# Two-step weight transfers, four token-halved projection units and a split step 1 in a one-core SSM + GeGLU kernel

## The chip, the cores and the metric

One core of a Trainium2 chip. The metric is the device time of one execution in microseconds (us), the median over several executions. Every execution also has a **span**: from the program's first instruction to its last, as the trace has it. Time less span is what lies outside.

Engines in profile lines: PE is TensorE, PEld its weight loads, DVE VectorE, ACT ScalarE, POOL GpSimd, SP SyncE, whose queue issues almost all transfers.

## The reference, cut to what matters

```python
x  = A_x                                   # (1, 2048, 512), bf16
xn = layernorm(x)                          # over the 512 columns
# A: a diagonal complex recurrence over the 2048 tokens
Bu = xn @ B_bar.T                          # the "B projection", 512 complex states
h_t = Lam_bar * h_{t-1} + Bu_t
y  = 2 * Re(h @ C.T) + xn * Dskip
# B: gated feed-forward, F = 1376
f  = (gelu(xn @ w_gate) * (xn @ w_up)) @ w_down
out = x + y + f
```

The kernel works on four blocks of 512 tokens, each of four 128-token tiles. A contraction over 512 columns takes four steps k = 0 to 3 of 128.

## The kernel before

A list of operations goes through a small scheduler in the program. It keeps the written order on TensorE and SyncE and sorts VectorE, ScalarE and GpSimd by its own model of time, so a change in one place can reorder those three.

The head: block 0 is computed from centred, not yet normed tiles, so that TensorE can start as soon as one tile and one weight step are there. SyncE sends tile x0, then single weight steps of 128 KB, with x2 and x3 between:

```python
def ld_wk(W, Wc, src, k):                                  # one step of one matrix
    f0, f1 = FC[0]                                         # columns 0 to 511
    return S.dma(lambda e: e.dma_start(W.ap[:, k, f0:f1], src[128*k:128*(k+1), f0:f1]),
                 256*(f1-f0), writes=[Wc[k]], tag="ld_w")
...
ld_x0(0)
GATE["par"] = S.order_behind(ld_x0(1, "scalar", [wrm]), GATE["table"])   # x1 on ScalarE's queue
for k in range(KD):
    if k in (1, 3):
        ld_x0((k + 3) // 2)
    ld_wk(WG, WGc, ins["B_w_gate"], k)
    ld_wk(WU, WUc, ins["B_w_up"], k)
ld_w(WG, WGc, ins["B_w_gate"], 1); ld_w(WU, WUc, ins["B_w_up"], 1)
... # then the last columns, the transpose of the parameters, the transposes of block 0
```

TensorE's order in the head; `ks(k, tile, which)` does step k of a tile for gate (0), up (1) or both, and `cent_T` transposes a centred tile:

```python
ks(0, 0, [0], True); ks(0, 0, [1])
cent_T(1, 1, 4, 7)
ks(0, 1, [0], True); ks(0, 1, [1])
ch(*stats(0, 2)); ch(sub(2))          # VectorE: statistics and centring of tile 2
ks(1, 0, [0, 1])                      # step 1 of tile 0
cent_T(2, 0, 1, 6); cent_T(2, 1, 4, 7)   # transposes of tile 2
ks(1, 1, [0, 1])
...
```

Later, the B projection of block 1 waits for the four transposes of that block's normed tiles. Its first units start on the first two tiles:

```python
def BU(b, halved=0):
    ...
    for unit_ in units[:halved]:
        mm(*unit_, 0, 2)                       # tokens 0 to 255
    for n, (c, s, bank) in enumerate(units):
        mm(c, s, bank, 2 if n < halved else 0, 4)   # the rest, or the whole unit
        ...                                    # eviction on ScalarE
...
BU(0); CHAIN(0, 2); H0_T()
BU(1, 2)
```

## Time and profile before

| | before |
|---|---|
| median of the first 3 runs | 177.25 us (176.85 to 177.71) |
| the execution whose trace the prediction read | 177.77 us, span 176.5 |
| TensorE busy | 97% |
| holes in TensorE's stream after 4.7 us, in that trace | 0.61 us and 0.72 us |

The profile lines, and how they are read, stand in the prediction.

### The profile page before, as it was taken

The page shows a single profiled execution, that of the slowest core. Times are in us where ns is not written, and L with a number is a line of the kernel's source. Part 1 is how long each engine was busy: PE and PEld are TensorE (multiplying, and loading weights), DVE is VectorE, ACT ScalarE, POOL GpSimd, SP SyncE. Part 2 cuts the span into 40 slices and gives each one's busy share as a digit, 9 for nine tenths or more (in the row PEclk, how much of TensorE's full clock was granted, in tenths as well). Part 3 has the DMA queues.
Part 4 walks back from the last instruction along what each step waited for, and adds up shares of the span by engine and source line. Part 5 has one row for each costly group of instructions (what it writes and reads, how often), then busy time and mean ns, then how long its engine had stood idle before and what let it go on. Part 6 is the DMA issues. An engine that isn't in the chain of part 4 may idle for free.

```text
span 176.5 us, 2485 instructions
## 1 busy us (share of the span) xinstructions
PE 172.0 (97%) x866; PEld 83.9 (48%) x881; DVE 159.8 (91%) x278; ACT 95.0 (54%) x187; POOL 9.8 (6%) x24
## 2 busy tenths in 40 slices
PE   8899999899999999999999999999999999999995
PEld 3545564544644444444644444444464444444454
DVE  6886999995999999879999999999999999999941
ACT  5464768799876899265676693000657970000000
POOL 3122040202000000000100000000000000000000
DMA  5899999895899000001134000002001000000312
GB/s 152 222 332 174 240 146 194 142 134 105 177 263 295 0 4 2 0 30 59 33 61 89 0 0 0 4 0 87 32 0 30 4 0 0 0 0 0 119 63 61
DMA packets 32420, 14.36 MB, mean 81 GB/s; under 512 B 23736, under 2 KB 32408, under 8 KB 32408
## 3 DMA queue, kind: packets, MB, share of 16 engines
q1 hardware_dynamic: 32240, 14.07, 36.7%
q8 instruction: 7, 0.11, 0.3%
q10 hardware_dynamic: 168, 0.13, 0.2%
q14 instruction: 5, 0.04, 0.1%
HBM read 6.46 MB, written 2.10 MB: 48 GB/s over the span
## 4 chain that ended last, share of the span: by engine, by line
PE 80%; DVE 6%; DMA 6%; SPq 4%; issue 2%; POOL 1%; DVEq 0%; POOLq 0%
PE PS L884 37%; PE PS L843 29%; PE PS L749 11%; DMA arena<-arena 6%; PE PS L817 2%; SPq L484 2%; DVE arena L599 1%; DVE arena L610 1%; SPq L489 1%; DVE arena L597 1%; DVE arena L629 1%; DVE arena L724 1%; SPq L493 1%; POOL arena L552 1%; DVE arena L864 0%
## 5 line engine op out<-in xcount | busy, mean ns | idle before, releaser
L884 PE MATMUL PS<-arena 128*128 128x512 bf16 (+3 forms) x317 | 65.9, 366 | 0.3
L843 PE MATMUL PS<-arena 128*128 128x512 bf16 x257 | 57.1, 379 | 0.4
L884 PEld LDWEIGHTS PS<-arena 128*128 128x128 bf16 (+1 forms) x323 | 30.8, 98 | 35.2
L843 PEld LDWEIGHTS PS<-arena 128*128 128x128 bf16 x264 | 25.8, 98 | 30.2
L787 DVE TENSOR_TENSOR_SCAN arena<-arena 128x512 bf16<-128x512 f32 x32 | 38.8, 1254 | 0.0
L858 ACT ACTIVATE arena<-PS 128x512 bf16<-128x512 f32 x33 | 19.8, 599 | 24.8 <-DVE arena L902 16.7
L749 PE MATMUL PS<-arena 128*128 128x512 bf16 (+1 forms) x134 | 28.2, 366 | 0.7 <-DMA arena<-arena 0.6
L862 ACT ACTIVATE arena<-PS 128x512 bf16<-128x512 f32 x33 | 19.8, 601 | 4.7 <-PE PS L843 4.7
L749 PEld LDWEIGHTS PS<-arena 128*128 128x128 bf16 x136 | 13.2, 98 | 14.9 <-DMA arena<-arena 0.8
L876 ACT ACTIVATE PS<-arena 128x512 f32<-128x512 bf16 (+2 forms) x17 | 9.6, 581 | 19.7 <-DVE arena L902 19.0
L758 ACT ACTIVATE arena<-PS 128x512 bf16<-128x512 f32 x32 | 17.6, 594 | 2.5 <-PE PS L749 2.5
L902 DVE TENSOR_TENSOR arena<-PS,arena 128x512 bf16<-128x512 f32 (+2 forms) x17 | 10.8, 652 | 6.3 <-PE PS L884 6.3
L864 DVE TENSOR_TENSOR arena<-arena 128x512 bf16<-128x512 bf16 x33 | 13.2, 417 | 2.2 <-ACT arena L862 2.0
L776 DVE TENSOR_TENSOR arena<-arena 128x4096 bf16<-128x4096 bf16 (+1 forms) x5 | 9.2, 1859 | 0.8 <-ACT arena L606 0.8
L774 DVE TENSOR_TENSOR arena<-arena 128x4096 bf16<-128x4096 bf16 (+1 forms) x5 | 9.2, 1859 | 0.3 <-ACT arena L605 0.3
L799 DVE TENSOR_TENSOR arena<-arena 128x4096 bf16<-128x4096 bf16 x4 | 9.1, 2287 | 0.1
L800 DVE TENSOR_TENSOR arena<-arena 128x4096 bf16<-128x4096 bf16 x4 | 9.1, 2283 | 0.0
L610 DVE BATCH_NORM_STATS2 arena<-arena 128x6 f32<-128x512 bf16 x12 | 7.7, 678 | 0.5 <-DMA arena<-in_A_x_dram 0.5
L721 ACT ACTIVATE arena<-PS,arena 128x256 bf16<-128x256 f32 (+1 forms) x16 | 6.1, 446 | 2.5 <-DVE arena L556 1.6
L712 PE MATMUL PS<-arena 128*128 128x512 bf16 (+1 forms) x40 | 7.1, 336 | 0.0
L724 DVE SCALAR_TENSOR_TENSOR arena<-PS,arena 128x256 bf16<-128x256 f32 (+1 forms) x16 | 6.3, 444 | 0.6 <-PE PS L701 0.6
L701 PE MATMUL PS<-arena 128*128 128x512 bf16 (+1 forms) x28 | 6.0, 348 | 0.4 <-issue 0.4
(95 smaller groups left out, 123.6 us busy)
## 6 DMA issues: line engine op xcount, KB each, us to landing
out_dram<-arena SPq DMA_DIRECT2D x15, 128.0 KB, 1.7
arena<-in_A_x_dram SPq DMA_DIRECT2D x3, 512.0 KB, 5.9
arena<-in_B_w_down_dram SPq DMA_DIRECT2D x1, 1280.0 KB, 7.0
arena<-in_B_w_gate_dram SPq DMA_DIRECT2D x4, 128.0 KB, 3.1
arena<-in_B_w_up_dram SPq DMA_DIRECT2D x4, 128.0 KB, 3.4
arena<-in_B_w_gate_dram SPq DMA_DIRECT2D x1, 480.0 KB, 6.9
arena<-in_B_w_up_dram SPq DMA_DIRECT2D x1, 480.0 KB, 7.8
arena<-arena SPq DMA_TRANSPOSE x25, 3.1
```

Of the source, the lines that this page charges most:

```text
L610: return (V(lambda e: e.bn_stats(ST[tt].ap, X[tt].ap), d_dve_1x(512), [X[tt]], [ST[tt]], "bnst"), V(lambda e: e.bn_aggr(MVt[b][j].ap, ST[t ...
L749: ins_ = e.matmul(PS[bank][:, 128 * j0:128 * j1], BBT[c][dk].ap[:, 128 * s:128 * (s + 1)], XNT[b].ap[:, dk, 128 * j0:128 * j1], start=(dk ...
L758: GATE["evBu"] = ACT(lambda e, bank=bank, k3=k3, s=s, c=c: e.activation(SSc[k3][s][c].ap, PS[bank][:, :], ACTF.Copy), d_act(512), [BANK[ba ...
L774: V(lambda e, s0=s0, s1=s1: e.tensor_tensor(TA.ap[:, s0:s1], ssb.ap[:, s0:s1], cos4[:, s0:s1], ALU.mult), d_dve_tt2x(1024 * step), [ss, CO ...
L787: V(lambda e, g=g, rb=rb, init=init: e.tensor_tensor_scan(g.ap, rb, g.ap, init, ALU.mult, ALU.add), d_dve_scan(512), [g, PA[RRr]] + ([CARc ...
L843: ins_ = e.matmul(PS[bank][0:m, c0:c1], W.ap[:, dk, 128 * ft:128 * ft + m], XNT[b].ap[:, dk, c0:c1], start=(dk == 0), stop=(dk == KD - 1))
L858: GATE["last_gelu"] = ACT(lambda e, bg=bg, kk=kk, m=m: e.activation(GG[kk].ap[0:m, :], PS[bg][0:m, :], ACTF.Gelu_apprx_tanh), d_act(512), ...
L862: ACT(lambda e, bu=bu, kk=kk, m=m: e.activation(UPB[kk].ap[0:m, :], PS[bu][0:m, :], ACTF.Copy), d_act(512), [BANK[bu]], [UPB[kk]], "evU")
L864: V(lambda e, kk=kk, m=m, ft=ft, k2=k2: e.tensor_tensor(HTt[k2][ft].ap[0:m, :], GG[kk].ap[0:m, :], UPB[kk].ap[0:m, :], ALU.mult), d_dve_tt ...
L876: ACT(lambda e: e.activation(PS[bank][:, c0:c1], X[tt].ap[:, c0:c1], ACTF.Copy), d_act(c1 - c0), [X[tt]], [BANK[bank]], "seed")
L884: ins_ = e.matmul(PS[bank][:, c0:c1], l_[:, 128 * j:128 * (j + 1)], r_[:, c0:c1], start=False, stop=last and n == len(ops) - 1, skip_group ...
L902: V(lambda e: e.tensor_tensor(OUTB[ko].ap[:, c0:c1], PS[bank][:, c0:c1], XD[tt].ap[:, c0:c1], ALU.add), d_dve_1x(c1 - c0), [BANK[bank], XD ...
```

## The change

Its intent: fewer issues on SyncE's queue, so that what comes behind the weights (parameters, transposes of blocks 0 and 1) starts earlier; more work for TensorE while the transposes of block 1 are on their way; and a start on step 1 with its gate half.

```diff
-def ld_wk(W, Wc, src, k):
+def ld_wk(W, Wc, src, k0, k1):            # steps k0 to k1-1 in one transfer, rearranged "(k p) f -> p k f"
...
-for k in range(KD):
-    if k in (1, 3):
-        ld_x0((k + 3) // 2)
-    ld_wk(WG, WGc, ins["B_w_gate"], k)
-    ld_wk(WU, WUc, ins["B_w_up"], k)
+ld_wk(WG, WGc, ins["B_w_gate"], 0, 2)
+ld_wk(WU, WUc, ins["B_w_up"], 0, 2)
+ld_x0(2)
+ld_wk(WG, WGc, ins["B_w_gate"], 2, 4)
+ld_wk(WU, WUc, ins["B_w_up"], 2, 4)
+ld_x0(3)
...
-ks(1, 0, [0, 1])
+ks(1, 0, [0])
+ks(1, 0, [1])
...
-BU(1, 2)
+BU(1, 4)
```

(The body of `ld_wk` is cut to a comment; the rest is whole.)

More of the change, by code (lines that the diff above doesn't have):

```diff
@@ L480, in ld_x @@
                 512 * 1024, writes=X[4 * b:4 * b + 4], tag="ld_x%d" % b)
-        def ld_wk(W, Wc, src, k):
+        def ld_wk(W, Wc, src, k0, k1):
             f0, f1 = FC[0]
-            return S.dma(lambda e: e.dma_start(W.ap[:, k, f0:f1], src[128 * k:128 * (k + 1), f0:f1]),
-                         256 * (f1 - f0), writes=[Wc[k]], tag="ld_w")
+            return S.dma(lambda e: e.dma_start(W.ap[:, k0:k1, f0:f1], src[128 * k0:128 * k1, f0:f1].rearrange("(k p) f -> p k f", p=128)),
+                         256 * (k1 - k0) * (f1 - f0), writes=Wc[k0:k1], tag="ld_w")
         def ld_w(W, Wc, src, n):
```

## The prediction

> **What bounds the kernel now.** I read the page's busy table and the chain that ended last, then TensorE's order of time, then the wait of each gap in it, then the DMA queue's order of time.
>
> Busy table and chain, of the page (share of the span 176.5 us):
>
> ```profile
> PE 172.0 (97%) x866; PEld 83.9 (48%) x881; DVE 159.8 (91%) x278; ACT 95.0 (54%) x187; POOL 9.8 (6%) x24
> ...
> PE 80%; DVE 6%; DMA 6%; SPq 4%; issue 2%; POOL 1%; DVEq 0%; POOLq 0%
> ```
>
> TensorE is busy 97% and carries 80% of the chain. A busy row says little about pipelined matmuls, so I went through TensorE's starts one by one. Next to one another, matmuls of 512 columns start 216 ns apart and those of 256 columns 109 ns. Against that spacing there are only two holes between 4.7 us and the end, apart from five gaps of exactly one matmul (0.216 us), which I take for missing records. They stand in the order of time (start, length, last column: idle before and what ended it):
>
> ```profile
> 5.33 0.60 PE L701 MATMUL PS<-arena 128*128 128x256 bf16 x4
> 6.38 0.59 PE L701 MATMUL PS<-arena 128*128 128x512 bf16 x2 [0.45 <-issue]
> ...
> 24.56 7.94 PE L749 MATMUL PS<-arena 128*128 128x512 bf16 x39
> 33.06 6.21 PE L749 MATMUL PS<-arena 128*128 128x256 bf16 x31 [0.56 <-DMA arena<-arena]
> ```
>
> The rows show modelled ends that include the drain. Start to start, hole 1 is 6.376 - 5.655 - 0.109 = 0.61 us, hole 2 is 33.061 - 32.233 - 0.109 = 0.72 us. After 33.06 us TensorE's stream is dense for 141.5 us, to 174.6. So whatever reaches 33 us earlier or later moves the end by the same amount, and a change that adds no work can win at most 0.61 + 0.72 = 1.33 us, or 0.75%. That already settles most of the question at a 2% mark.
>
> Who ends the holes? Hole 1 is the wait for the up half of weight step 1. The DMA view of the window 3.0 to 3.2 us has it (size, us from issue to landing); issued at 3.08, it landed at 6.28, and the matmul starts at 6.38:
>
> ```profile
> arena<-in_B_w_up_dram SPq DMA_DIRECT2D x1, 128.0 KB, 3.2
> ```
>
> Hole 2 is the wait for the transposes of block 1: issued at 24.89, 26.13, 27.46 and 29.17, they landed at 30.86, 31.36, 32.35 and 32.92.
>
> The queue's order of time, head and what follows, shows the cost of issuing:
>
> ```profile
> 5.45 0.44 SPq L484 DMA_DIRECT2D arena<-in_B_w_up_dram  x1
> ...
> 8.20 2.81 SPq L510 DMA_TRANSPOSE arena<-arena  x1
> 11.06 5.18 SPq L736 DMA_TRANSPOSE arena<-arena  x4
> 16.28 0.58 SPq L478 DMA_DIRECT2D arena<-in_A_x_dram  x1
> 16.91 3.09 SPq L521 DMA_TRANSPOSE arena<-in_A_B_re_dram  x1
> ```
>
> One load occupies the queue for 0.47 us, whether 128 or 384 KB. And VectorE, which the block-1 transposes depend on, has one hole there:
>
> ```profile
> 16.92 0.16 DVE L553 TENSOR_TENSOR arena<-arena 128x4 f32<-128x4 bf16 x1 [1.46 <-POOL arena L552]
> ```
>
> POOL's instruction waited for the parameter transpose, issued at 8.20 and landed at 15.66 behind the weights.
>
> **What the Trainium skill says.** "DMA: Bandwidth & Descriptors", Rules for kernel authors, advises coalescing small transfers, and its Anatomy section puts a fixed cost of about 2 us on a DMA, most of it the write receipt. The trace agrees on the size: the first 128 KB load took 2.2 us to land, the first weight load 2.4. The same page, Queues, rings and completion order, says descriptors on each DMA engine are consumed in ring order. So a tile issued behind larger weights starts after their bytes; landings in the head do follow issue order in this trace. "TensorE: Matmul & The Clock Gate", Back-to-back issue gap, gives N / 2.4 + 2.5 ns for warm matmuls: 216 and 109 ns, exactly what the trace has.
>
> **The change part by part.**
>
> (a) Four halved units instead of two. Before, eight 256-column matmuls on tokens 0 to 255 ran from 31.47 to 32.34, and then TensorE waited for transposes 3 and 4. With four units there are sixteen, 16 x 0.109 = 1.74 us, to 33.21 if the start is the same. The last transpose landed at 32.92, plus the 0.14 us seen from landing to matmul, so at 33.06: hole 2 closes whole. Cost: eight 512-column matmuls become sixteen of 256, 8 x (2 x 109 - 216) = 16 ns. The PSUM banks are free: the evictions of units 0 to 3 of block 0 ended by 28.81. Sum: -0.70 us.
>
> (b) Loads. Before, the queue sends x0, WG0, WU0, x2, WG1, WU1, WG2, WU2, x3, WG3, WU3; now x0, WG01, WU01, x2, WG23, WU23, x3. Four issues go, 4 x 0.474 = 1.9 us of queue time. Hole 1 must vanish as such: step 1 arrives with step 0. But x2 now lies behind 256 KB more. TensorE's next work after step 1 of tile 0 is the transpose of tile 2, and it needs x2, its statistics and its centring. In the trace x2 landed at 5.11 and the centred tile was done at 6.43, so 1.32 us later. With 0.04 to start, the tile-2 transposes can't start before X + 1.36, X being the new landing of x2. They started at 6.81. The head therefore gains 5.45 - X, capped at the 0.61 of hole 1 (with x2 unmoved it would be 0.34), and loses if X is later than 5.45.
>
> What is X? Bytes ahead of and with x2 (the second tile, from the other queue, included) grow from 640 to 896 KB. Packets in the trace reach 640 KB at 4.4 us and 896 KB at 5.3, and landing follows 0.7 us or more behind. The stretches of one microsecond (last columns: DMA share, GB/s) show how full the engines were:
>
> ```profile
> 2.00:3.00 1.00, 1.00 (x4) 0.43 (x3) 0.39 (x2) 0.21 (x2) 0.36 (x2) 1.00 1.00 342
> 3.00:4.00 1.00, 1.00 (x6) 0.33 (x5) 0.96 (x3) 0.72 (x2) 0.00 (x0) 1.00 0.67 167
> 4.00:5.00 1.00, 1.00 (x11) 0.73 (x10) 0.59 (x3) 0.46 (x3) 0.00 (x0) 1.00 0.90 308
> 5.00:6.00 1.00, 0.93 (x10) 0.60 (x8) 0.83 (x2) 0.95 (x3) 0.00 (x0) 1.00 0.88 190
> ```
>
> Only the stretch from 3 to 4 us has room, a third of it: at 342 GB/s, 0.33 x 342 = about 113 KB. If the larger transfers fill it, 896 KB are moved when 783 were, at about 4.85, and X is about 5.6 (4.85 + 0.75). If they fill nothing, X is about 6.1; if the engines kept 342 from 2 us on, it is 4.7 + 0.7 = 5.4. My middle is 5.6: the head loses 0.15 us.
>
> (c) The gate half of step 1 alone. Two 512-column matmuls become four of 256: 4 ns. Both halves of step 1 lie in transfers that the step 0 matmuls have already waited for, so I expect no gain from it.
>
> (d) The queue is freed 1.9 us earlier, but the parameter transpose that follows held it 2.81 us with the weights still draining, so I count 0.5 to 1 us for what comes behind it. VectorE's 1.46 us hole shrinks, so block 1 is normed and transposed earlier too. That only matters for hole 2, closed by (a) anyway. It counts nothing more.
>
> Sum: -0.70 + 0.15 = -0.55 us. Before, the median was 177.25, so **176.7 us**.
>
> **Rivals.** First: x2 lands much later (6.1 to 6.3). For it speak latencies growing from 2.2 to 3.7 us over the head, a sign of a backlog that larger transfers do not cure. Against it, the 0.67 share. Head loss 0.65 to 0.85, total about 177.25 to 177.4: no change. Second: the loads run at full rate and the head gains up to 0.3; then the halves would also come earlier, and TensorE would need transposes 1 and 2 of block 1 before 31.36. If they move with the queue, the total is about 176.2; if not, that gain turns into a wait ahead of the halves, and it is 176.55. Third: a new order on VectorE and ScalarE, since the program's own list scheduler sorts them again, opens a stall. Against it: block 0's states, ready at 69.8, are first needed near 74.1 (64.6 plus 44 matmuls of 216 ns), 4 us of slack; the first reused bank of block 1's projections is free at 44.1 and needed at 45.8. A microsecond of disorder is absorbed; 177.5 at worst.
>
> **Range and chances.** The mechanisms span 176.2 to 177.5, and three runs before spread over 0.9 us. 8 in 10: **176.0 to 177.5**. Faster by over 2% needs 3.5 us, and the holes hold 1.33: 0.01. Slower by over 2% needs a stall that nothing here shows: 0.015. Within 2%: 0.975.
>
> **What would show it.** Right: no TensorE idle before the second token halves of block 1, and thirty-two 256-column matmuls there; four weight loads of 256 KB with x2 landing near 5.6; idle ahead of the tile-2 transposes instead of ahead of step 1; parameter transpose landed before 15.66. Wrong: a new wait of over 0.5 us after 33 us, x2 after 6.3, block 1's transposes landing after 33.1, or a different dense length after the projections.

## The result, and the profile after

| | before | changed |
|---|---|---|
| median of 6 runs | 177.26 us (176.85 to 177.71) | 178.03 us (177.67 to 178.37) |
| span of the traced execution | 176.5 | 176.4 |
| time less span | 1.26 to 1.37 over 33 runs in later sessions | 1.67 to 1.78 over 6 runs |

The ratio is 1.0041, with a 95% interval of 1.0020 to 1.0063. A ratio is the mean time of one kernel's fast runs over that of the other's of the same rounds, so it is not quite the ratio of the medians. The changed kernel is **0.4% slower**, inside 2%, but outside the predicted range of 176.0 to 177.5, and with the other sign.

The odd thing first: the two traced spans are equal, yet the times of these two executions differ by 0.4 us (177.77 and 178.18). So part of the loss is not in the span at all.

The page of the changed kernel, busy row and chain:

```profile
PE 172.1 (98%) x876; PEld 85.0 (48%) x891; DVE 160.1 (91%) x278; ACT 95.3 (54%) x187; POOL 11.9 (7%) x24
...
PE 94%; DMA 2%; DVE 1%; SPq 1%; issue 1%
```

TensorE now carries 94% of the chain: the wait for transposes in the middle is gone from it. In TensorE's order of time (start, length, form, count, then idle before and its cause):

```profile
4.75 0.39 PE L702 MATMUL PS<-arena 128*128 128x256 bf16 x2
5.72 0.39 PE L702 MATMUL PS<-arena 128*128 128x256 bf16 x2 [0.58 <-DMA arena<-in_B_w_up_dram]
5.95 0.33 PE L680 MATMUL PS<-arena 128*128 128x128 bf16 x3
6.12 1.04 PE L702 MATMUL PS<-arena 128*128 128x256 bf16 x8
7.38 0.40 PE L680 MATMUL PS<-arena 128*128 128x128 bf16 x4 [0.23 <-DVE arena L951]
7.62 2.97 PE L702 MATMUL PS<-arena 128*128 128x512 bf16 x13
...
25.15 11.21 PE L750 MATMUL PS<-arena 128*128 128x512 bf16 x65
```

The wait ahead of step 1 is gone. In its place stand two others: 0.74 us start to start ahead of the up half of step 0, and 0.39 us ahead of the tile-2 transposes (the brackets show less, since modelled ends include the drain). In the kernel before, the same rows were:

```profile
6.81 0.38 PE L679 MATMUL PS<-arena 128*128 128x128 bf16 x4
7.03 2.97 PE L701 MATMUL PS<-arena 128*128 128x512 bf16 x13
```

The block of 13 large matmuls begins at 7.62 instead of 7.03 us: the head loses **0.59 us**. Against that, the projections run from 25.15 through with no hole. The last matmul starts at 174.26 instead of 174.36, a net gain of 0.10 us on this pair of traces.

VectorE shows who held the tile-2 transposes, and the DMA view of the window 2.1 to 2.2 us when its input came (size, us from issue to landing; issued at 2.17, so landed at 6.00):

```profile
6.03 0.69 DVE L611 BATCH_NORM_STATS2 arena<-arena 128x6 f32<-128x512 bf16 x1 [1.33 <-DMA arena<-in_A_x_dram]
```

```profile
arena<-in_A_x_dram SPq DMA_DIRECT2D x1, 128.0 KB, 3.8
```

In the kernel before, x2 was issued at 2.12 and landed at 5.11 (window 2.1 to 2.3 us):

```profile
arena<-in_A_x_dram SPq DMA_DIRECT2D x1, 128.0 KB, 3.0
```

The stretches of one microsecond (last two columns: DMA share, GB/s) show that the larger transfers did fill the gap from 3 to 4 us, 286 GB/s where the kernel before had 167; from 2 to 3 us they moved less, 284 for 342:

```profile
2.00:3.00 1.00, 1.00 (x4) 0.43 (x3) 0.52 (x2) 0.22 (x2) 0.36 (x2) 1.00 0.94 284
3.00:4.00 1.00, 1.00 (x6) 0.44 (x5) 0.96 (x3) 0.62 (x2) 0.00 (x0) 1.00 1.03 286
4.00:5.00 1.00, 1.00 (x10) 0.60 (x7) 0.51 (x3) 0.59 (x5) 0.00 (x0) 1.00 0.97 296
5.00:6.00 1.00, 0.42 (x5) 0.26 (x4) 0.00 (x0) 0.45 (x2) 0.00 (x0) 1.00 1.01 326
```

More bytes moved by 6 us, and still a later start: bandwidth was not what the head wanted.

SyncE's queue shows the issues saved, and what became of them:

```profile
5.88 0.86 SPq L489 DMA_DIRECT2D arena<-in_B_w_up_dram  x1
6.87 2.24 SPq L511 DMA_TRANSPOSE arena<-arena  x1
10.97 5.15 SPq L737 DMA_TRANSPOSE arena<-arena  x4
```

The parameter transpose is issued 1.3 us earlier (6.87 for 8.20) and lands at 13.36 instead of 15.66, but block 0's transposes start at 10.97 instead of 11.06. They wait for tile 0 to be normed, and VectorE, held up by x2, is 0.9 us later there. The first of them lands 2.2 us earlier (13.71 for 15.88), the last only 0.1 (17.36 for 17.47), and what the queue issues next starts 0.1 us earlier (16.17 for 16.28).

### The profile page after: what moved, and what is told of

It reads as the page before. It is cut to its first block, busy times and chain, and to the rows that moved or that the text cites. A ratio compares the mean times of both kernels' runs of the same rounds, so it can differ in the third digit from the quotient of the medians.

```text
span 176.4 us, 2498 instructions
## 1 busy us (share of the span) xinstructions
PE 172.1 (98%) x876; PEld 85.0 (48%) x891; DVE 160.1 (91%) x278; ACT 95.3 (54%) x187; POOL 11.9 (7%) x24
## 4 chain that ended last, share of the span: by engine, by line
PE 94%; DMA 2%; DVE 1%; SPq 1%; issue 1%
PE PS L885 37%; PE PS L844 32%; PE PS L750 16%; PE PS L713 4%; PE PS L818 3%; PE PS L702 2%; DMA arena<-in_A_x_dram 2%; SPq L484 0%; DVE arena L611 0%; PE PS L680 0%; SPq L493 0%; DVE arena L951 0%; DVE arena L903 0%; DVE arena L612 0%
## 5 line engine op out<-in xcount | busy, mean ns | idle before, releaser
L844 PEld LDWEIGHTS PS<-arena 128*128 128x128 bf16 x264 | 25.7, 98 | 30.3
L750 PEld LDWEIGHTS PS<-arena 128*128 128x128 bf16 x144 | 14.1, 98 | 13.3
```

Of the source, the lines that this page charges most:

```text
L750: ins_ = e.matmul(PS[bank][:, 128 * j0:128 * j1], BBT[c][dk].ap[:, 128 * s:128 * (s + 1)], XNT[b].ap[:, dk, 128 * j0:128 * j1], start=(dk ...
L844: ins_ = e.matmul(PS[bank][0:m, c0:c1], W.ap[:, dk, 128 * ft:128 * ft + m], XNT[b].ap[:, dk, c0:c1], start=(dk == 0), stop=(dk == KD - 1))
```

## The experiments

Three questions: where the 0.4 us outside the span come from, what the head loses and why, and what the four halves are worth.

**1. The loads without the four halves.**

```diff
 # the changed kernel
-BU(1, 4)
+BU(1, 2)
```

> The changed kernel with two halved B-projection units instead of four; VectorE's and ScalarE's order is then that of the kernel before. Theory (the head's bytes): x2 lands near 6.0 us and the 13 large matmuls after the tile-2 transposes start near 7.62 instead of 7.03, a loss of 0.59 us; the block-1 transposes land near 32.3 to 32.9, and TensorE, later by 0.59, ends its eight half matmuls at 32.93, so the wait ahead of the second halves shrinks from 0.72 to under 0.2. Span 176.4 to 176.6, so the four halves add little to these loads. Rival (the halves alone hid the wait): the wait stays at 0.7 and the span is near 177.1. Time outside the span: if the 0.5 us that the changed kernel has there come with its loads, they are here; if with the number of TensorE instructions, they are not.

Measured: median 177.84, ratio 1.0031 (1.0012 to 1.0049). In its trace, which is of the longest of the six runs, x2 landed at 6.41 and the up half of step 0 at 6.07, later than expected; the 13 large matmuls started at 8.02. The wait ahead of the second token halves is 0.20 us, where the rival had 0.7. Mean span of six runs 176.28, as in the changed kernel (176.32). So **with these loads the two more halves add next to nothing**. Time less span is 1.68 to 1.78: it comes with the loads, not with the number of TensorE's instructions or the orders on VectorE and ScalarE, which are here those of the kernel before (the traces have the same sequences).

**2. The four halves alone.**

```diff
 # the kernel before
-BU(1, 2)
+BU(1, 4)
```

> The kernel before with four halved B-projection units and nothing else. Theory: hole 1 (0.61 us ahead of step 1) stays, hole 2 (0.72 us ahead of the second token halves) closes, span 175.75 to 175.85, 0.70 us below the kernel before. Rival: the new order of VectorE and ScalarE, which the four halves bring with them, moves the wait elsewhere, and the span is above 176.2. Time less span: 1.3 us as before if the loads made the difference, 1.7 if the instruction counts did.

Measured: median 177.38 beside 177.37 of the kernel before; ratio 0.9994 (0.9973 to 1.0015). The trace has no hole left at all, hole 1 included, and a span of 175.6; but the six spans run from 175.5 to 176.9 with a median of 176.05, and those of the kernel before in the same session have a median of 176.0. Both theories miss: the hole was closed, and nothing was won. A gain of 0.70 us would be a ratio of 0.9961, below the interval. VectorE and ScalarE run in the order of the changed kernel here, so that order costs nothing that can be seen either. That made me doubt the hole. Time less span is 1.28 to 1.33.

**3. x2 on the other queue.**

```diff
 # the changed kernel
 GATE["par"] = S.order_behind(ld_x0(1, "scalar", [wrm]), GATE["table"])
+GATE["par"] = S.order_behind(ld_x0(2, "scalar", [wrm]), GATE["par"])
...
-ld_x0(2)
```

> The changed kernel with tile x2 sent from ScalarE's queue behind x1, ahead of the large weight transfers. Theory (bytes bound, not the queue's order alone): x2 lands before 4.8 us and no longer gates, but the up half of steps 0 and 1 then has 896 KB ahead of and with it and lands near 5.7 to 6.1, so TensorE waits 0.8 to 1.1 us there and the tile-2 transposes start near 7.1 to 7.4; the head still loses 0.3 to 0.6 us against the kernel before; span 176.0 to 176.4. Rival (x2's place in the queue is the whole cause): the head gains 0.3 to 0.6 us against the kernel before and the span is 175.1 to 175.5.

Measured: median 177.87, ratio 1.0043 (1.0011 to 1.0075). The up half of step 0 landed at 5.92, TensorE waited 1.03 us for it, the tile-2 transposes started at 7.23; the median span is 176.3 (five runs 176.1 to 176.7, one 178.3). As the theory has it: with 896 KB to move ahead of the last one needed, taking x2 forward only moves the wait to the weights. One number missed: x2 itself, issued at 1.43, landed at 5.37 and not before 4.8.

**4. Single first steps, x2 on the other queue.**

```diff
 # experiment 3
-ld_wk(WG, WGc, ins["B_w_gate"], 0, 2)
-ld_wk(WU, WUc, ins["B_w_up"], 0, 2)
+for k in range(2):
+    ld_wk(WG, WGc, ins["B_w_gate"], k, k + 1)
+    ld_wk(WU, WUc, ins["B_w_up"], k, k + 1)
```

> As e3, but steps 0 and 1 of both weights in transfers of one step (128 KB) and steps 2 and 3 in one of two, four halved units, gate half of step 1 alone. Theory: the first up half lands near 4.9 to 5.1, step 1's gate half near 5.4 and up half near 5.8; TensorE's waits before the tile-2 transposes add to under 0.3 us, those start near 6.3 against 6.81; no wait before the second token halves; span 175.1 to 175.4 (both holes of 1.33 us gone). Rival: the transposes 1 and 2 of block 1 become the gate and give 0.3 to 0.5 us back, span 175.5 to 175.8.

Measured: median 177.95, ratio 1.0026 (1.0010 to 1.0042). A miss: x2 landed at 5.42 and pushed the first up half, single again, to 5.64; TensorE waited 0.70 us there. Mean span 176.10, no better than before. Time less span 1.78 to 1.87, another value again.

**5. The changed kernel with a longer SyncE program.** Time less span had been 1.31 in kernels with 82 SyncE instructions in the trace, 1.71 with 78, 1.55 with 77 (experiment 3) and 1.83 with 79 (experiment 4). So I lengthened the program where SyncE idles:

```diff
 # the changed kernel, where the program emits its waits
+if op is self.out_ops[4]:                 # ahead of the fifth store
+    for _ in range(4):
+        h.wait_ge(*waits[-1])             # a wait that is already fulfilled
```

> The changed kernel with four more waits, already fulfilled, on SyncE ahead of its fifth store, where it idles: its count of instructions in the trace goes from 78 back to 82, that of the kernel before. Theory (the 0.4 us outside the span hang on the length of SyncE's program, not on the loads): time less span falls from 1.67 to 1.78 to about 1.33, the span stays at 176.0 to 176.6, and the median time is near 177.6. Rival (the loads themselves leave something open at the end): time less span stays at 1.7, median 178.0.

Measured: time less span **1.35 to 1.41**, from 1.67 to 1.78, with nothing else altered. Only two of the four waits appear in the trace: 80 instructions, not 82. The median is 177.8, ratio 1.0032, since the mean span of these six is 176.47. The loads leave little or nothing open at the end: 0.33 of the 0.40 us go when SyncE's program has two more instructions in the trace.

**6. Halves and gate half on the loads of before.**

```diff
 # the kernel before
-ks(1, 0, [0, 1])
+ks(1, 0, [0])
+ks(1, 0, [1])
...
-BU(1, 2)
+BU(1, 4)
```

> The kernel before with its loads of single steps, with four halved units and with the gate half of step 1 of tile 0 alone. Theory: with single transfers the gate half lands 0.3 to 0.85 us ahead of the up half, so it can run first and hole 1 shrinks by up to 0.22 us; the second hole is closed; span 175.4 to 175.9, time less span 1.33, median 177.0. Rival (the head's landing times vary from run to run by as much): no difference from e2, median 177.3.

Measured: median 177.17 beside 177.29; ratio 0.9996 (0.9982 to 1.0009). The rival: no difference that can be told from the scatter. In its trace TensorE ran at half speed until 6.5 us (see experiment 11), so there was no wait ahead of step 1 for the split to shorten.

**7. The kernel before with four more waits.** The edit of experiment 5 on the kernel before.

> The kernel before with four more fulfilled waits on SyncE (82 to 86 instructions). Theory (length of SyncE's program): time less span moves away from 1.33 by 0.1 us or more, in a direction I can't tell, with the span unchanged at 175.9 to 176.5. Rival: 1.33 stays. The run also gives a second trace of the head of the kernel before: I expect the two holes to be there in other sizes, 0.3 to 0.7 each, as spans of its runs lie between 175.9 and 176.5.

Measured: median 177.15, ratio 0.9993 (0.9981 to 1.0005); time less span 1.25 to 1.33, not moved. That part of the theory fell: a longer program does not always shift it. Together the counts give 77: 1.55, 78: 1.71 to 1.73 (three kernels), 79: 1.83, 80: 1.38 and 1.39 (two kernels with different loads), 82: 1.30 to 1.32, 84: 1.29 and 1.31. It rises by 0.1 to 0.2 per instruction up to 79 and then drops; the kernels of this row differ in other ways too, and only experiments 5 and 7 change the count alone.

The second half of the expectation was worth more. TensorE in this trace of what is, in the head and the middle, the kernel before:

```profile
4.75 1.01 PE L704 MATMUL PS<-arena 128*128 128x256 bf16 x4
5.55 0.52 PE L682 MATMUL PS<-arena 128*128 128x128 bf16 x3
5.88 1.39 PE L704 MATMUL PS<-arena 128*128 128x256 bf16 x6
7.10 0.39 PE L682 MATMUL PS<-arena 128*128 128x128 bf16 x4
7.32 2.97 PE L704 MATMUL PS<-arena 128*128 128x512 bf16 x13
...
24.86 11.41 PE L752 MATMUL PS<-arena 128*128 128x512 bf16 x59
```

The last row has the projections of blocks 0 and 1 in one piece: **there is no second hole**, with two halved units only. The transposes of block 1 landed at 29.25 to 31.88 instead of 30.86 to 32.92.

**8. The same bytes ahead of x2, in single transfers.**

```diff
 # the changed kernel
-ld_wk(WG, WGc, ins["B_w_gate"], 0, 2)
-ld_wk(WU, WUc, ins["B_w_up"], 0, 2)
+for W, Wc, nm in ((WG, WGc, "B_w_gate"), (WU, WUc, "B_w_up")):
+    for k in range(2):
+        ld_wk(W, Wc, ins[nm], k, k + 1)
```

> The changed kernel with the first two transfers of two steps split into four of one step in the same order of bytes (gate 0, gate 1, up 0, up 1, then x2). Theory (bytes ahead): x2 still lands at 5.9 to 6.4 us, the tile-2 transposes start at 7.3 to 7.7 as in the changed kernel; the up half of step 0 lands at 5.0 to 5.5, so the wait for it shrinks to under 0.5 us but the one for x2 grows. Span 176.2 to 176.7. Rival (the size of a transfer is what costs): x2 lands before 5.5 and the span falls to 175.9 or less.

Measured: median 178.22, ratio 1.0055 (1.0042 to 1.0068), mean span 176.86. TensorE's order of time:

```profile
4.74 0.40 PE L703 MATMUL PS<-arena 128*128 128x256 bf16 x2
5.38 0.39 PE L703 MATMUL PS<-arena 128*128 128x256 bf16 x2 [0.24 <-DMA arena<-in_B_w_up_dram]
5.61 0.33 PE L681 MATMUL PS<-arena 128*128 128x128 bf16 x3
5.78 1.04 PE L703 MATMUL PS<-arena 128*128 128x256 bf16 x8
7.39 0.40 PE L681 MATMUL PS<-arena 128*128 128x128 bf16 x4 [0.57 <-DVE arena L952]
```

x2 landed at 6.01 us, to a hundredth where the two-step transfers put it (6.00), and the tile-2 transposes start at 7.39 for 7.38. The view of the window 3.05 to 3.1 us has the tile, issued at 3.10:

```profile
arena<-in_A_x_dram SPq DMA_DIRECT2D x1, 128.0 KB, 2.9
```

The size of the transfers is not what delays the tile. **It is the 896 KB ahead of and with it** instead of 640. One thing missed: the mean span is 0.54 us longer than that of the changed kernel, above the expected 176.2 to 176.7. In the trace 0.29 us of it are two more gaps, after 8.7 and 10.4 us; the up half of steps 2 and 3 landed at 8.97 instead of 7.40. So nothing here speaks against two-step transfers as such.

**9. A version made from what was learned.** Single steps 0 and 1 with x2 in its old place, two-step transfers for 2 and 3 only, four halves, gate halves of two tiles first, and eight more waits on SyncE.

```diff
 # the changed kernel, and the waits of experiment 5, eight of them
-ld_wk(WG, WGc, ins["B_w_gate"], 0, 2)
-ld_wk(WU, WUc, ins["B_w_up"], 0, 2)
-ld_x0(2)
+for k in range(2):
+    ld_wk(WG, WGc, ins["B_w_gate"], k, k + 1)
+    ld_wk(WU, WUc, ins["B_w_up"], k, k + 1)
+    if k == 0:
+        ld_x0(2)
...
 ks(1, 0, [0])
+ks(1, 1, [0])
 ks(1, 0, [1])
 cent_T(2, 0, 1, 6); cent_T(2, 1, 4, 7)
-ks(1, 1, [0, 1])
+ks(1, 1, [1])
```

> Single transfers for steps 0 and 1 with x2 where the kernel before has it, transfers of two steps for 2 and 3 only, x3 after them, four halved units, the gate halves of step 1 of tiles 0 and 1 ahead of their up halves, and eight fulfilled waits on SyncE to keep its program at 80 or more. Theory: x2 lands near 5.1 with 640 KB ahead of and with it; the wait for step 1's up half falls under 0.3 us; two issues fewer bring the block-1 transposes forward; no second hole; span 175.5 to 175.8, time less span 1.3 to 1.4, median 176.9, faster than the kernel before by 0.1 to 0.3%. Rival: the new orders on VectorE and ScalarE, or steps 2 and 3 landing after 8.4 us, give it back; span 176.0 and over, no gain.

Measured: median 177.76, ratio 1.0034 (1.0012 to 1.0055), mean span 176.53, time less span 1.26 to 1.36. The rival: x2 landed at 5.54 instead of 5.1; the wait for step 1 is gone, but the up half of steps 2 and 3 landed at 8.42 and the stream has small gaps of 0.15 and 0.16 us around there. The orders on VectorE and ScalarE also changed, and the trace does not say which of the two costs most. It beats neither the kernel before nor experiment 6.

**10. The kernel before, once more.** Unchanged, one look. A single run has no state; its clock was 1.0.

> The kernel before, unchanged, for a second trace. Theory (the trace that the prediction read was of an off-median execution, its second hole larger than is usual): the transposes of block 1 land at 30 to 32.3 us instead of 32.92 and the wait ahead of the second token halves is under 0.4 us; span 175.7 to 176.2. Rival: the hole is again 0.6 to 0.8 us.

Measured: 177.10, span 175.8. The transposes landed at 29.52 to 31.65, and again there is no second hole:

```profile
6.05 0.59 PE L701 MATMUL PS<-arena 128*128 128x512 bf16 x2 [0.15 <-issue]
6.67 0.40 PE L679 MATMUL PS<-arena 128*128 128x128 bf16 x4
6.91 3.03 PE L701 MATMUL PS<-arena 128*128 128x512 bf16 x13
...
24.51 11.84 PE L749 MATMUL PS<-arena 128*128 128x512 bf16 x62
```

Hole 1 is 0.32 us start to start, with another 0.19 ahead of the tile-2 transposes. The trace that the prediction read was that of a longer execution than most. The record shows where its second hole came from: in all three traces of this kernel (this one, experiment 7 and the one read) the first transpose of block 1 landed 0.57 to 0.60 us after the 512 KB block of x issued ahead of it, at 28.95, 28.65 and, in the trace read, 30.29 us.

**11. The changed kernel without the gate half.**

```diff
 # the changed kernel
-ks(1, 0, [0])
-ks(1, 0, [1])
+ks(1, 0, [0, 1])
```

> The changed kernel with step 1 of tile 0 in one piece again. Theory: no difference from the changed kernel, as both halves of step 1 come with transfers that step 0 has already waited for: span 176.0 to 176.7, time less span 1.7 as SyncE's program is as long, median 177.8 to 178.1. Rival (the split costs or gains): more than 0.3 us either way.

Measured: median 178.22, ratio 1.0068 (1.0023 to 1.0114). Four of the six spans are 176.0 to 176.6, as the theory has it; two are 178.1 and 178.6 (the latter with a granted clock of 0.99). The traced one is of those two, and its head is of another kind:

```profile
5.93 0.61 PE L702 MATMUL PS<-arena 128*128 128x256 bf16 x2 [0.60 <-DMA arena<-in_B_w_up_dram]
6.33 0.53 PE L680 MATMUL PS<-arena 128*128 128x128 bf16 x3
6.65 1.91 PE L702 MATMUL PS<-arena 128*128 128x256 bf16 x6
8.36 0.63 PE L680 MATMUL PS<-arena 128*128 128x128 bf16 x4
8.79 3.47 PE L702 MATMUL PS<-arena 128*128 128x512 bf16 x13
```

Up to 8.79 us most matmuls of 256 columns start 213 ns apart, twice the usual 109. The page "TensorE: Matmul & The Clock Gate" of the Trainium skill, Part 1, describes this: TensorE starts at half its clock and is released after a busy window that runs freely, so the moment varies from run to run. The traces agree that half speed comes first and that its end varies, but by far more than the 500 ns either way that the page gives: before 4.9 us in seven of the thirteen, by 6.6 in five, and near 9.8 here, where the first large matmuls still start 427 ns apart. Whether the wait of 0.9 us inside the window delayed the release is not settled by this one trace. Nor is it settled whether these loads make long executions likelier: three of 47 runs with two-step transfers have spans over 177.5 us (here and in experiment 3), none of 52 with the loads of before. On the gate half: no gain or loss seen in the four ordinary runs, and the interval is too wide for more.

## Why the prediction was wrong, point by point

**The value of the four halves, -0.70 us: wrong.** The mechanism is real: in the traces with four halves, on the old loads or the new, the wait ahead of the second token halves is gone. But hole 2 was 0.72 us in one execution, and absent in the two other traces of the kernel before (experiments 7 and 10). Over six runs the halves alone gave 0.9994. The step that failed is the first: the holes were measured in a trace of 177.77 us and then taken off a median of 177.25. An execution 0.5 us above the median should have been suspected of having just such a hole. The interval of experiment 2, from 0.48 us faster to 0.27 slower, leaves no room for 0.70.

**The landing of x2, 5.6 us, and the head's loss of 0.15: right mechanism, two terms too small.** The prediction had 896 KB moved by about 4.85 us. Counting the packets of SyncE's and ScalarE's queues in the trace, the one that completes 896 KB starts at 5.03: the stretch from 3 to 4 us was filled as forecast (286 GB/s), but the one from 2 to 3 fell to 284. From there to landing the prediction added 0.75 us. Measured it is 6.00 - 5.03 = **0.98 us** (before rounding), and with the same loads elsewhere 1.06 (experiment 5), 1.23 (experiment 11) and 1.49 (experiment 1). For x2 at 640 KB behind single transfers it is 0.60 to 0.93 in six traces. The trace that the prediction read held a warning: the up half of step 1, which completes 896 KB there, landed 0.98 us after its count (6.28 for 5.30). In experiment 8 the count came later (5.36) and the landing sooner after it (0.64), to the same 6.01. So the count over all engines does not give one tile's landing alone; that some engines run ahead into later transfers is my reading, since the trace does not name the engines. The rest of the head follows the prediction's formula: x2 + 1.36 = 7.36, and the transposes started at 7.38. The wait of 0.74 us ahead of the up half of step 0 was not forecast at all; it did not decide, since the wait for x2 ended later, but it did in experiment 3, where x2 came forward. The head lost 0.59 us against the trace predicted from, 0.71 against experiment 10 (7.62 for 6.91).

**The gate half: right.** It was expected to do nothing.

**The freed queue, 0.5 to 1 us for what comes behind: wrong in the size.** The four issues saved less than the 1.9 us forecast: issues in the head took up to 0.51 us each instead of 0.47, and the parameter transpose was issued 1.33 us earlier. The parameters landed 2.3 us earlier and VectorE's hole of 1.46 us is gone, but block 0's transposes started only 0.09 us earlier, as they wait for a VectorE that waits for x2. Against experiments 7 and 10, where they started at 10.55 and 10.60, they are later, and so are block 1's: landed at 30.29 to 32.30 for 29.52 to 31.65 in experiment 10. It was not counted in the sum.

**What was not in the sum at all: the time outside the span.** Removing four issues shortened SyncE's program from 82 to 78 instructions, and time less span went from 1.31 to 1.71. Experiment 5 shows it: two more instructions on the same loads give 1.38; experiment 8, other loads with the same 80, gives 1.39. An instruction fetch is a candidate: the last 8 KB instruction transfer starts 0.4 us after the last counted instruction in the kernel before and 1.1 us after it in the changed one. But the other traces do not follow it in order: 1.3 us in experiment 3 and 1.1 in experiment 4, where the time outside is 1.55 and 1.83. Why the cost rises to 79 and drops at 80 stays open; that a fetch boundary in the closing code is crossed is not shown.

**The account.** Mean span: 176.32 over six runs of the changed kernel, 175.99 over the 33 of the kernel before (other sessions, on three chips; their mean time, 177.30, is that of the six runs beside the changed kernel too), so +0.33. Outside: +0.40. Together +0.73 us; the ratio of 1.0041 is 0.0041 x 177.26 = 0.73 us. The predicted sum was -0.70 + 0.15 = -0.55. The miss of 1.28 us is 0.70 for the halves, if they are worth nothing in typical executions, 0.18 for the head (+0.33 for 0.15; single pairs of traces have 0.6 to 0.7), and 0.40 that no engine's stream shows.

**The rivals.** "x2 lands much later" is the one that came nearest: it named 6.1 to 6.3 us for x2 and a head loss of 0.65 to 0.85, and it erred by taking hole 2 as won. The second, loads at full rate, fell with x2 at 6.00. A new order on VectorE and ScalarE opened no stall in the changed kernel, and experiment 2, with the same order, lost nothing.

## What to carry to other kernels

Before a hole in a trace is counted as a gain, compare the traced execution's time with the median of the others, and look at a second trace: a hole that comes from transfer timing may be gone. When transfers are merged, ask of every tile behind them how many bytes now lie ahead of it, and what engine stands waiting for it; the sum of bytes, not the size of the transfers, decided here. And compare time with span: four instructions less on a nearly idle engine went with 0.40 us here, outside everything that a view of the engines shows, and two more took 0.33 of it back.

## What the Trainium skill lacked or had wrong

- "DMA: Bandwidth & Descriptors", Rules for kernel authors, recommends merging small transfers (its row names 64 KB; the loads here have 128); it does not say that a small tile behind the merged ones pays. Here x2 went from 5.11 to 6.00 us with 896 instead of 640 KB up to its end, and just as late (6.01) in single transfers of the same order.
- The same page's fit of about 2.0 us plus bytes over 436 GB/s, measured on GpSimd's path, gives 2.6 us for 256 KB; the page has no such fit for SyncE's queue. From that queue in this head the first 256 KB took 3.5 us and the second 4.0, with other transfers beside them; a 128 KB tile 2.0 to 2.3 when first.
- "TensorE: Matmul & The Clock Gate", Back-to-back issue gap, gives 131 ns per matmul of 512 columns for streams with a weight load each, and calls 216 ns the isolated gap. Here such a stream, each matmul with its weight load, runs at 216 ns throughout, and at 109 for 256 columns.
- No page has it that the time after a program's last instruction depends on the length of an engine's program: 1.31 us with 82 instructions on SyncE, 1.71 with 78, 1.83 with 79, 1.38 with 80 (the counts are those of the trace; the cause is open).
